# A Strassen-like mixing product: outer sums, weight conversions and loads at planned steps, stores of converted weights on GpSimd's queue, and ScalarE squares in the first block of the last stage

## The chip, the cores and the metric

One core of one Trainium2 chip runs the whole program in one launch. The metric is the device time of an execution in microseconds. Engines are named as the profile does: PE is TensorE (PEld its weight load), DVE is VectorE, ACT is ScalarE, POOL is GpSimd, SP is SyncE, which here only issues DMAs.

## The reference

Three layers follow each other on x of 4 x 3072 x 256.

```python
X = np.fft.rfft(x, axis=1)                      # layer 1: mixing in frequency
Yr = Xr @ w_r - Xi @ w_i + b_r; Yi = Xr @ w_i + Xi @ w_r + b_i
y = irfft(soft_threshold(Yr, Yi, 0.01))
h = np.maximum(x @ w_in, 0.0); u, v = h[..., :512], h[..., 512:]   # layer 2
v_n = (v - mu) / np.sqrt(var + 1e-06)
v_s = np.einsum('ts,bsd->btd', w_spatial, v_n) + b_spatial[None, :, None]
x = (u * v_s) @ w_out
h = x @ w2_in                                    # layer 3
out = (s * np.maximum(h, 0) ** 2 + b) @ w2_out   # w2_in 256 x 2048, w2_out 2048 x 256
```

The einsum with w_spatial (3072 x 3072) against 3072 rows of 4 x 512 columns is the mixing product. The weights of layers 2 and 3 come as 64-bit numbers and have to be converted.

## The kernel before

The program has three stages on TensorE: the frequency layer with the first product of layer 2 (up to some 540 us), the mixing product (to 1811 us), and the last stage, which makes the rest of layer 2 and layer 3 in 24 blocks of 512 columns. All products are done as float32 pairs: ScalarE rounds an operand to its high part, VectorE subtracts to get the low part (called *lows* below), and three passes (high by high, high by low, low by high) go to TensorE.

**The mixing product** (`mixing`, L731) uses Winograd's form of Strassen's scheme twice. The outer scheme has seven products, in the order 1, 5, 2, 6, 3, 7, 4 (`OUTER`, L708); each is again split into quarters a11 to a22 and b11 to b22 of six tiles each, and seven inner products in the order 2, 5, 3, 1, 6, 7, 4 (`INNER`, L717). An inner product runs over NS = 6 contraction tiles. So there are 7 x 7 x 6 = 294 **steps** n, each of 24 matmuls of 128 x 384 columns on four accumulators of two banks (`multiply`, L848). A step is named here by its number; steps 42 to 83 are those of the second outer product, and step 71 is the last of its fifth inner product.

An a tile (128 x 768) and a b tile (128 x 512) of a quarter lie in SBUF and are changed in place by the inner scheme's sums (`sums`, L803, on VectorE, three steps ahead). `high` (L831, ScalarE) and `low` (L836, VectorE) split them two steps ahead. When the last step of an inner product ends, `evacuate` (L866) takes the four accumulators out: VectorE adds an accumulator to a kept tile (called a **fold** below, L874) and POOL's queue stores it to md, or ScalarE copies it to a kept tile (L878). The next step writes the same accumulators, so TensorE waits for it.

A tile that has had its last use is loaded anew for the next outer product. `freed` lists it; `loads` (L782) issues on SyncE's queue the load of the **first term** (L766), and for outer products 5, 6, 3, 7 and 4 of a **second term** (L772) into a staging tile (`st_a`, `st_b`, three buffers each). After three steps `outer_sums(3)` (L796) lets VectorE add or subtract the second term in place, and where OUTER says so (products 5 and 6, the second and fourth in the list) POOL's queue stores the sum for later use (L777).

**Conversions.** 40 halves of the weights of the last stage are converted during the mixing product (`convert_half`, L1254, and `convert`, L133): SyncE loads the 64-bit half into a staging tile, VectorE works nine instructions, ScalarE one, and SyncE's queue stores the result (L162). They take staging buffers of the same `st_a` (raw and result) and `st_b` (three work tiles). In the loop of `run` a conversion is taken up where nothing is to be added or loaded, and worked off in one piece:

```python
            outer_sums(3)
            if conversion and (todo or n % 3 == 2):
                conversion.pop()()
            loads()
            if n >= 6 and not conversion and not added and not todo and n % 3 == 0:
                conversion = [x for x in [convert_half(stage)] if x]
```

Each engine, and each DMA queue, works in the order in which this code issues; nothing is reordered later.

**The last stage** (`output`) goes over blocks n and over k = 0 to 7 in `layer1` (L1080): 12 matmuls to ps_h, ScalarE's relu to r (L1094), VectorE's square (L1095), ScalarE's rounding (L1096) and VectorE's low part (L1097). Two steps later `layer2` uses it. Ahead of it `u_product`, `gate` (L1053 to L1058) and `out_product` of the next block are put in at k = 4 to 6. In block 0 VectorE also adds up the columns of the second weight (`add_columns`, L1132).

Of the kernel before, what the change touches and what calls it, by code (L numbers as in the profile page):

```python
# [27 lines left out]
NS = TQ // 128  # L28
# [7 lines left out]
def f(ap):  # L36
    return ap.bitcast(F32)
# [94 lines left out]

def convert(nc, tile_, raw, dst, n):  # L133

# [26 lines left out]
    def s4():  # L161
        nc.sync.dma_start(out=dst, in_=f(o))  # L162
    return [s0, s1, s2, s3, s4]
# [558 lines left out]


class Stage:

# [5 lines left out]
def mixing(tc, nc, ws, vn, md, sd, convert_half):  # L731
# [7 lines left out]
    q = {}  # L739
# [23 lines left out]
    def load(g, name, i):  # L763
        first, then = OUTER[outer[g]][0 if name[0] == "a" else 2:][:2]
        t = q[name, i]
        nc.sync.dma_start(out=t, in_=source(first, name, i))  # L766
        if then is None:
            return
        op, second, kept = then
        n = t.shape[1]  # L770
        s = banks[2].tile([128, n], F32, tag="st_" + name[0], name="st_" + name[0], bufs=3)
        nc.sync.dma_start(out=s, in_=source(second, name, i))  # L772

        def add():
            nc.vector.tensor_tensor(out=t, in0=t, in1=s, op=getattr(ALU, op))
            if kept:
                nc.gpsimd.dma_start(out=sd[kept][int(name[1]) - 1, int(name[2]) - 1, i], in_=t)  # L777
        added.append((now[0], name[0], add))

    todo = []  # L780

    def loads():  # L782

        n = {"a": 3, "b": 3}
        for _, kind, _ in added:
            n[kind] -= 1
        for x in sorted(todo):
            g, _, i, name = x
            if OUTER[outer[g]][1 if name[0] == "a" else 3] is not None:
                if n[name[0]] <= 0:  # L790
                    continue
                n[name[0]] -= 1
            todo.remove(x)
            load(g, name, i)

    def outer_sums(age):  # L796
        while added and added[0][0] <= now[0] - age:
            added.pop(0)[2]()

# [3 lines left out]
    def sums(n):  # L803

        p, i = INNER[n // NS % 7], n % NS
        a11, a12, a21, a22, b11, b12, b21, b22 = (q.get((x, i)) for x in QUARTERS)
        if p == 2:
# [89 lines left out]
    def run():  # L897
# [12 lines left out]
        for n in range(total):  # L910
# [15 lines left out]
            if ends:  # L926
                evacuate(n, 2)
                evacuate(n, 3)
            outer_sums(3)
            if conversion and (todo or n % 3 == 2):  # L930
                conversion.pop()()
            loads()
            if n >= 6 and not conversion and not added and not todo and n % 3 == 0:
                conversion = [x for x in [convert_half(stage)] if x]
        while True:
            for x in conversion:
                x()
            conversion = [x for x in [convert_half(stage)] if x]
            if not conversion:
                break  # L940
        left.close()
# [10 lines left out]
def output(tc, nc, yd, md, chunks, cd, bs, s_in, b_in, out, finish):  # L952
# [127 lines left out]
    def layer1(n, k):  # L1080
# [13 lines left out]
        nc.scalar.activation(r, ps, AF.Relu)  # L1094
        nc.vector.tensor_mul(r, r, r)  # L1095
        nc.scalar.copy(s[:, 0], r)  # L1096
# [144 lines left out]
def network(ctx, tc, ins, out):  # L1241
# [12 lines left out]
    def convert_half(pool):  # L1254

        if not halves:
            return None
        j, h = halves.pop(0)
        src = chunks[j]
        src = src[:, h, :] if len(src.shape) == 3 else src[:, h * 256:(h + 1) * 256]  # L1260

        def c_tile(tag, shape, dtype):
            tag, bufs = ("st_a", 3) if tag in ("raw", "o") else ("st_b", 3)
            return pool.tile(shape, dtype, tag=tag, name="c_w", bufs=bufs)
        raw = convert_load(nc, c_tile, src, 256)
        return lambda: [step() for step in convert(nc, c_tile, raw, cd[j][:, :, h * 256:(h + 1) * 256], 256)]
    with tc.manual_schedule():
# [29 lines left out]
```

## Time and profile before

| | before |
|---|---|
| median of 3 runs | 3144.45 us (3143.99 to 3144.72) |
| profiled execution, its own time | 3143.22 us |
| span of its profile | 3141.5 us |
| PE busy | 3035.7 us (97%) |
| DVE busy | 2289.4 us (73%) |
| ACT busy | 1395.2 us (44%) |
| POOL busy | 387.9 us (12%) |
| granted clock of TensorE, mean | 0.988 |

The span is the time from the first to the last instruction of the profiled execution. Busy shares are averages over the three stages; TensorE's is near 100% in the settled parts of the last two, so what can be saved there is what a stretch takes beyond its matmuls. The granted clock is a share of 2.4 GHz; where it is 0.5 TensorE ran at 1.2 GHz.

### The profile page before, as it was taken

The page shows a single profiled execution, that of the slowest core. Times are in us where ns is not written, and L with a number is a line of the kernel's source. Part 1 is how long each engine was busy: PE and PEld are TensorE (multiplying, and loading weights), DVE is VectorE, ACT ScalarE, POOL GpSimd, SP SyncE. Part 2 cuts the span into 40 slices and gives each one's busy share as a digit, 9 for nine tenths or more (in the row PEclk, how much of TensorE's full clock was granted, in tenths as well). Part 3 has the DMA queues.
Part 4 walks back from the last instruction along what each step waited for, and adds up shares of the span by engine and source line. Part 5 has one row for each costly group of instructions (what it writes and reads, how often), then busy time and mean ns, then how long its engine had stood idle before and what let it go on. Part 6 is the DMA issues. An engine that isn't in the chain of part 4 may idle for free.

```text
span 3141.5 us, 42065 instructions
## 1 busy us (share of the span) xinstructions
PE 3035.7 (97%) x16026; PEld 2744.0 (87%) x16026; DVE 2289.4 (73%) x3291; ACT 1395.2 (44%) x2069; POOL 387.9 (12%) x488
## 2 busy tenths in 40 slices
PE   6999997999999999999999989999999999999999
PEld 4889885999999999999999978888888888888887
DVE  5888998797878888888878866566565665655664
ACT  5777766433334333434434324344343434334343
POOL 2665544021000210000000000000000000000000
PEclk8999999999999999999999999999999999999999
DMA  8987768586456957467471621202111211102010
GB/s 242 287 288 242 236 215 289 185 330 264 157 194 217 353 214 231 143 209 276 141 256 40 241 101 49 83 31 74 57 61 44 76 42 60 71 31 101 31 37 14
DMA packets 217602, 488.01 MB, mean 155 GB/s; under 512 B 21748, under 2 KB 66616, under 8 KB 217400
## 3 DMA queue, kind: packets, MB, share of 16 engines
q1 hardware_dynamic: 185624, 358.23, 34.1%
q0 software_dynamic: 31776, 127.11, 11.0%
q8 instruction: 125, 2.05, 0.3%
q14 instruction: 77, 0.63, 0.1%
HBM read 322.72 MB, written 162.53 MB: 154 GB/s over the span
## 4 chain that ended last, share of the span: by engine, by line
PE 61%; issue 19%; DVE 11%; DMA 5%; ACT 2%; POOL 1%; SPq 0%; POOLq 0%; ACTq 0%; DVEq 0%
PE oacc L1111 16%; PE ps_h L1090 16%; PE acc L857 13%; PE ps_o L1070 4%; PE ps_u L1045 4%; PE ps_m L414 3%; PE ps_vp L579 2%; PE ps_z L340 1%; POOL md L875 1%; DMA st_b<-vn 1%; PE ps_g L367 1%; DMA c_w<-in_moe_w_in_dram 1%; DMA st_a<-in_moe_w_spatial_dram 1%; DVE a_hl L838 1%; DVE bn L592 1%
## 5 line engine op out<-in xcount | busy, mean ns | idle before, releaser
L857 PE MATMUL acc<-a_hl,b_hl 128*128 128x384 f32 x7056 | 1238.8, 336 | 32.8 <-DVE kept L874 12.0
L857 PEld LDWEIGHTS acc<-a_hl,b_hl 128*128 128x128 f32 x7056 | 1233.0, 189 | 38.6 <-ACT kept L878 12.8
L1090 PE MATMUL ps_h<-x_hl,w 128*128 128x512 f32 x2304 | 555.9, 390 | 6.2 <-ACT r L1094 6.2
L1111 PE MATMUL oacc<-q_hl,w 128*128 128x512 f32 x2304 | 555.1, 390 | 1.6 <-ACT q_hl L1096 0.8
L1090 PEld LDWEIGHTS ps_h<-x_hl,w 128*128 128x128 f32 x2304 | 434.3, 189 | 97.0 <-ACT r L1094 6.6
L1111 PEld LDWEIGHTS oacc<-q_hl,w 128*128 128x128 f32 x2304 | 433.3, 188 | 92.1 <-ACT q_hl L1096 1.2
L834 ACT CAST a_hl<-a 128x768 fp32r<-128x768 f32 x253 | 211.6, 836 | 522.3 <-PE acc L857 443.8
L1095 DVE TENSOR_TENSOR r<-r 128x1024 f32<-128x1024 f32 x192 | 234.9, 1224 | 214.8 <-ACT r L1094 214.1
L1097 DVE TENSOR_TENSOR q_hl<-r,q_hl 128x1024 fp32r<-128x1024 f32 x192 | 235.2, 1225 | 214.3 <-ACT q_hl L1096 214.3
L1094 ACT ACTIVATE r<-ps_h 128x1024 f32<-128x1024 f32 x192 | 197.1, 1027 | 325.9 <-PE ps_h L1090 325.9
L838 DVE TENSOR_TENSOR a_hl<-a,a_hl 128x768 fp32r<-128x768 f32 x253 | 241.3, 954 | 137.4 <-ACT a_hl L834 137.0
L1096 ACT CAST q_hl<-r 128x1024 fp32r<-128x1024 f32 x192 | 201.6, 1050 | 287.5 <-DVE r L1095 287.5
L838 DVE TENSOR_TENSOR b_hl<-b,b_hl 128x512 fp32r<-128x512 f32 x295 | 201.9, 685 | 0.0
L834 ACT CAST b_hl<-b 128x512 fp32r<-128x512 f32 x295 | 181.8, 616 | 0.0
L875 POOL DMA_DIRECT2D md<-kept x112 | 60.5, 540 | 828.9 <-DVE kept L874 824.5
L579 PE MATMUL ps_vp<-win,y_hl 128*128 128x512 f32 x576 | 149.8, 396 | 1.6 <-ACT y_hl L479 1.2
L1045 PE MATMUL ps_u<-y_hl,w 128*128 128x512 f32 x576 | 138.2, 389 | 0.0
L1070 PE MATMUL ps_o<-g,w 128*128 128x512 f32 x576 | 135.2, 390 | 1.7 <-DVE m L1053 0.8
L1070 PEld LDWEIGHTS ps_o<-g,w 128*128 128x128 f32 x576 | 107.9, 188 | 25.5 <-DVE m L1053 1.5
L1045 PEld LDWEIGHTS ps_u<-y_hl,w 128*128 128x128 f32 x576 | 108.2, 188 | 22.4
L579 PEld LDWEIGHTS ps_vp<-win,y_hl 128*128 128x128 f32 x576 | 101.2, 189 | 20.2 <-ACT y_hl L479 1.6
L414 PE MATMUL ps_m<-w_hi,xh 128*128 128x256 f32 x376 | 106.4, 283 | 8.6 <-DVE mt L426 8.6
(142 smaller groups left out, 3657.5 us busy)
## 6 DMA issues: line engine op xcount, KB each, us to landing
a<-in_moe_w_spatial_dram SPq DMA_DIRECT2D x144, 384.0 KB, 5.0
b<-vn SPq DMA_DIRECT2D x168, 256.0 KB, 5.4
md<-kept POOLq DMA_DIRECT2D x112, 384.0 KB, 5.6
m<-md SPq DMA_DIRECT2D x42, 1024.0 KB, 6.5
st_a<-in_moe_w_spatial_dram SPq DMA_DIRECT2D x72, 384.0 KB, 6.7
vn<-vr POOLq DMA_DIRECT2D x96, 256.0 KB, 4.4
s<-a POOLq DMA_DIRECT2D x48, 384.0 KB, 5.8
x_f<-in_x_dram SPq DMA_DIRECT2D x32, 384.0 KB, 6.3
```

What stands on the lines that cost most here:

```text
L414: nc.tensor.matmul(ps[:, n, :], lhs, rhs[:, ri, h, :], start=c == 0, stop=False)
L579: nc.tensor.matmul(ps, y[:, a, k, o:o + 128], win[k][:, w, :], start=c == 0, stop=c == 5)
L834: nc.scalar.copy(s[:, 0, :], t)
L838: sub(s[:, 1, :], term.pop((kind, n)), f(s)[:, 0, :])
L857: nc.tensor.matmul(acc[d][:, h, 0:TH], b[:, m, d * 128:(d + 1) * 128], a[:, w, h * TH:(h + 1) * TH], start=fresh and i == 0 and c == 0, st ...
L1045: nc.tensor.matmul(ps[:, d, 0:TB], win[k][:, a, o:o + 128], y[:, w, k, :], start=c == 0, stop=c == 5)
L1070: nc.tensor.matmul(ps[:, h, 0:TB], wo[k // 2][:, a, o:o + 128], g[:, w, k, :], start=c[h] == 0, stop=c[h] == 11, skip_group_check=n == 0)
L1090: nc.tensor.matmul(ps[:, e, 0:TB], w[:, a, o:o + 128], x[:, i, j, :], start=c == 0, stop=c == 5)
L1095: nc.vector.tensor_mul(r, r, r)
L1096: nc.scalar.copy(s[:, 0], r)
L1097: nc.vector.tensor_sub(s[:, 1], r, f(s)[:, 0])
L1111: nc.tensor.matmul(ps[:, h, 0:TB], w[:, a, o:o + 128], s[:, i, e, :], start=ff == 0 and c == 0, stop=ff == 2 * NP - 1 and c == 2)
```

## The change

In the mixing product the rule of the loop is replaced by tables of steps. `CONVERSIONS` lists the 40 steps after which a half is converted (42 times the outer product's place, 6 times the inner one's, and the tile); its load is issued when one of the next four steps is in the list. `ADD_AT` gives for each quarter the step at which its outer sum is made, counted from the start of the outer product before (so 42 and more lie in the outer product that uses it). First terms are loaded as soon as a tile is free. Second terms are loaded from `LEAD` = 3 steps before their sum, as staging buffers are free, in the order of those steps. The store of a converted half goes to GpSimd's queue. In the last stage ScalarE squares r in block 0, VectorE in the other blocks as before.

```diff
-def convert(nc, tile_, raw, dst, n):
+def convert(nc, tile_, raw, dst, n, queue=None):
...
-        nc.sync.dma_start(out=dst, in_=f(o))
+        (queue or nc.sync).dma_start(out=dst, in_=f(o))
...
+CONVERSIONS = {42 * g + 6 * p + i for g, p, i in (
+    (0, 1, 1), (0, 1, 3), (0, 1, 4), (0, 2, 1), (1, 2, 1), (1, 2, 4), (1, 3, 0), (1, 3, 1),
...
+ADD_AT = {"a12": 18, "b21": 30, "a21": 36, "b12": 36, "a22": 42, "b11": 42, "b22": 45, "a11": 48}
+LEAD = 3
...
         if then is None:
-            return
+            state[name, i] = g
+        else:
+            second_terms.append((g, name, i, then))
+
+    def load_second(g, name, i, then):
...
-        added.append((now[0], name[0], add))
+        added.append((g, name, i, add))
...
+    def due(g, name, i):
+        return 42 * (g - 1) + ADD_AT[name] + i
...
+        for x in sorted(second_terms, key=lambda x: due(*x[:3])):
+            g, name, i, _ = x
+            if n[name[0]] > 0 and now[0] >= due(g, name, i) - LEAD:
                 n[name[0]] -= 1
-            todo.remove(x)
+                second_terms.remove(x)
+                load_second(*x)
+        for g, _, i, name in sorted(todo):
             load(g, name, i)
...
-    def outer_sums(age):
-        while added and added[0][0] <= now[0] - age:
-            added.pop(0)[2]()
+        todo.clear()
+
+    def outer_sums(everything=False):
+        for x in list(added):
+            g, name, i, add = x
+            if everything or due(g, name, i) <= now[0]:
+                added.remove(x)
+                add()
+                state[name, i] = g
...
-            outer_sums(3)
-            if conversion and (todo or n % 3 == 2):
+            outer_sums()
+            if n in CONVERSIONS:
+                outer_sums(True)
                 conversion.pop()()
-            loads()
-            if n >= 6 and not conversion and not added and not todo and n % 3 == 0:
-                conversion = [x for x in [convert_half(stage)] if x]
...
+            loads(len(conversion))
+            if not conversion and any(m in CONVERSIONS for m in range(n + 1, n + 5)):
+                conversion.append(convert_half(stage))
...
-        nc.vector.tensor_mul(r, r, r)
+        if n == 0:
+            nc.scalar.square(r, r)
+        else:
+            nc.vector.tensor_mul(r, r, r)
...
-        return lambda: [step() for step in convert(nc, c_tile, raw, cd[j][:, :, h * 256:(h + 1) * 256], 256)]
+        return lambda: [step() for step in convert(nc, c_tile, raw, cd[j][:, :, h * 256:(h + 1) * 256], 256, nc.gpsimd)]
```

How the instructions stand. First SyncE's queue at the end of the first outer product, where the quarters of product 5 come in (b22 are first terms, L766 before and L779 now; st_a and st_b second terms, L772 before and L790 now). Before:

```order
L766 DMA b22_6341<-vn3_72 128x512
L772 DMA st_b_9163<-vn1_70 128x512
L766 DMA b22_6342<-vn3_72 128x512
L772 DMA st_b_9166<-vn1_70 128x512
L766 DMA b22_6343<-vn3_72 128x512
L772 DMA st_b_9211<-vn1_70 128x512
```

and now, from the last first terms on:

```order
L779 DMA a22_6340<-in_moe_w_spatial_dram 128x768
L779 DMA b22_6346<-vn3_72 128x512
L790 DMA st_b_9136<-vn0_69 128x512
L790 DMA st_a_9138<-in_moe_w_spatial_dram 128x768
L790 DMA st_b_9182<-vn0_69 128x512
L790 DMA st_a_9184<-in_moe_w_spatial_dram 128x768
L790 DMA st_b_9224<-vn0_69 128x512
L790 DMA st_a_9226<-in_moe_w_spatial_dram 128x768
```

Before, a first term and its second term alternate, so that the next first term stands behind a load that needs a staging buffer; now the first terms come early and the second terms of a22, b11, b22 and a11 follow by themselves.

Next VectorE ahead of the fold that ends step 71 (L838 and L869 are lows, L825 and L856 sums of the inner scheme, L874 and L905 folds). Before:

```order
L838 TENSOR_TENSOR a_hl<-a_6359,a_hl 128x768
L838 TENSOR_TENSOR b_hl<-b_6371,b_hl 128x512
L144 TENSOR_SCALAR c_w<-c_w 128x256
L145 TENSOR_SCALAR c_w<-c_w 128x256
L146 TENSOR_SCALAR c_w<-c_w 128x256
L149 TENSOR_SCALAR c_w<-c_w 128x256
L150 TENSOR_TENSOR c_w<-c_w 128x256
L151 TENSOR_SCALAR c_w<-c_w 128x256
L154 TENSOR_SCALAR c_w<-c_w 128x256
L155 SCALAR_TENSOR_TENSOR c_w<-c_w 128x256
L159 SCALAR_TENSOR_TENSOR c_w<-c_w 128x256
L825 TENSOR_TENSOR a_6361<-a_6337,a_6361 128x768
```

and now:

```order
L869 TENSOR_TENSOR a_hl<-a_6359,a_hl 128x768
L869 TENSOR_TENSOR b_hl<-b_6371,b_hl 128x512
L856 TENSOR_TENSOR a_6361<-a_6337,a_6361 128x768
L905 TENSOR_TENSOR kept<-acc,kept 128x768 x2
L869 TENSOR_TENSOR a_hl<-a_6360,a_hl 128x768
```

The conversion of nine instructions has left this place; before, the fold came right after the a-sum that closes the first list.

Last ScalarE at the start of block 0 of the last stage. Before:

```order
L1094 ACTIVATE r<-ps_h 128x1024
L1096 CAST q_hl<-r 128x1024
L1094 ACTIVATE r<-ps_h 128x1024
L1096 CAST q_hl<-r 128x1024
L1094 ACTIVATE r<-ps_h 128x1024
```

and now:

```order
L1120 ACTIVATE r<-ps_h 128x1024
L1122 ACTIVATE r<-r 128x1024
L1125 CAST q_hl<-r 128x1024
L1120 ACTIVATE r<-ps_h 128x1024
L1122 ACTIVATE r<-r 128x1024
```

The square stands on ScalarE's own list between relu and rounding, eight times; before, rounding waited there for VectorE.

## Rows read from the trace of the kernel before

**Rows 1.** Busy time in stretches; columns named in the first line.
```profile
core 0: us, PE busy (x) PEld busy (x) DVE busy (x) ACT busy (x) POOL busy (x), PEclk, DMA share, GB/s
1640.00:1743.00 103.00, 103.00 (x597) 103.00 (x596) 85.11 (x148) 44.58 (x68) 2.17 (x4) 1.00 0.21 69
...
693.35:737.42 44.07, 36.05 (x193) 35.12 (x193) 30.87 (x40) 13.95 (x20) 13.24 (x25) 0.92 1.03 415
1064.54:1109.21 44.67, 36.27 (x194) 35.34 (x193) 31.07 (x40) 13.95 (x20) 12.95 (x24) 0.92 1.03 414
833.11:898.10 64.99, 57.86 (x313) 56.93 (x313) 50.75 (x90) 21.86 (x34) 6.47 (x12) 0.95 0.65 213
1225.69:1238.77 13.08, 10.15 (x50) 9.69 (x49) 10.98 (x21) 3.01 (x5) 2.16 (x4) 0.87 0.60 199
...
1825.91:1886.69 60.78, 51.75 (x206) 40.75 (x204) 41.51 (x41) 18.19 (x19) 0.00 (x0) 0.89 0.12 43
1943.82:1998.22 54.40, 54.40 (x241) 45.06 (x240) 31.14 (x27) 22.03 (x22) 0.00 (x0) 1.00 0.18 63
```

**Rows 2.** Waits of PE, 693.35 to 737.42 us: total, times, longest.
```profile
PE acc L857 <- DVE kept L874: 5.3, 1, 5.3
```

**Rows 3.** Timeline of DVE: start, length, what; in brackets idle time and releaser.
```profile
729.52 0.69 DVE L775 TENSOR_TENSOR b<-b,st_b 128x512 f32<-128x512 f32 x1 [1.62 <-DMA st_b<-vn]
730.13 1.81 DVE L874 TENSOR_TENSOR kept<-acc,kept 128x768 f32<-128x768 f32 x2
731.87 0.95 DVE L838 TENSOR_TENSOR a_hl<-a,a_hl 128x768 fp32r<-128x768 f32 x1
732.73 0.69 DVE L838 TENSOR_TENSOR b_hl<-b,b_hl 128x512 fp32r<-128x512 f32 x1
733.33 0.95 DVE L874 TENSOR_TENSOR kept<-acc,kept 128x768 f32<-128x768 f32 x1
```

**Rows 4.** Timeline of all engines around the end of step 71.
```profile
853.50 0.42 SPq L129 DMA_DIRECT2D c_w<-in_moe_w_in_dram  x1
...
857.57 0.29 DVE L144 TENSOR_SCALAR c_w<-c_w 128x256 uint32<-128x256 uint32 x1 [2.12 <-DMA c_w<-in_moe_w_in_dram]
...
860.17 0.95 DVE L825 TENSOR_TENSOR a<-a,a 128x768 f32<-128x768 f32 x1
...
861.03 1.81 DVE L874 TENSOR_TENSOR kept<-acc,kept 128x768 f32<-128x768 f32 x2
...
862.13 6.16 PE L857 MATMUL acc<-a_hl,b_hl 128*128 128x384 f32 x26 [2.85 <-ACT a_hl L834]
```

**Rows 5.** Waits of SP's queue and of DVE, 540 to 1812 us.
```profile
SPq L162 <- DVE c_w L159: 443.7, 40, 26.2
...
DVE c_w L144 <- DMA c_w<-in_moe_w_in_dram: 16.7, 6, 4.9
```

**Rows 6.** DMA issues, 540 to 1812 us: count, KB each, median us to landing.
```profile
st_a<-in_moe_w_spatial_dram SPq DMA_DIRECT2D x72, 384.0 KB, 6.7
...
st_b<-vn SPq DMA_DIRECT2D x48, 256.0 KB, 6.1
```

**Rows 7.** Costliest groups of the page: count, busy us, mean ns, idle before.
```profile
L1095 DVE TENSOR_TENSOR r<-r 128x1024 f32<-128x1024 f32 x192 | 234.9, 1224 | 214.8 <-ACT r L1094 214.1
...
L1094 ACT ACTIVATE r<-ps_h 128x1024 f32<-128x1024 f32 x192 | 197.1, 1027 | 325.9 <-PE ps_h L1090 325.9
...
L875 POOL DMA_DIRECT2D md<-kept x112 | 60.5, 540 | 828.9 <-DVE kept L874 824.5
```

**Rows 8.** Timeline of all engines in block 0 of the last stage.
```profile
1856.71 1.22 DVE L1095 TENSOR_TENSOR r<-r 128x1024 f32<-128x1024 f32 x1
...
1861.53 1.22 DVE L1008 TENSOR_TENSOR m<-m,bias 128x1024 f32<-128x1024 f32 x1
1862.66 1.22 DVE L1053 SCALAR_TENSOR_TENSOR m<-ps_u,m 128x1024 f32<-128x1024 f32 x1
1863.91 1.04 ACT L1057 CAST g<-m 128x1024 fp32r<-128x1024 f32 x1 [4.89 <-DVE m L1053]
1864.86 1.02 ACT L1094 ACTIVATE r<-ps_h 128x1024 f32<-128x1024 f32 x1
...
1865.93 5.49 PE L1090 MATMUL ps_h<-x_hl,w 128*128 128x512 f32 x12 [6.18 <-ACT r L1094]
```

More of the change, by code (lines that the diff above doesn't have):

```diff
@@ L767, in load @@
         if then is None:
-            return
+            state[name, i] = g
+        else:
+            second_terms.append((g, name, i, then))
+    def load_second(g, name, i, then):
+        t = q[name, i]
         op, second, kept = then
@@ L777, in add, with loads @@
                 nc.gpsimd.dma_start(out=sd[kept][int(name[1]) - 1, int(name[2]) - 1, i], in_=t)
-        added.append((now[0], name[0], add))
+        added.append((g, name, i, add))
     todo = []
[L782 to L791, printed above, removed]
+    def due(g, name, i):
+        return 42 * (g - 1) + ADD_AT[name] + i
+    second_terms = []
+    def loads(taken):
+        n = {"a": 3 - taken, "b": 3}
+        for _, name, _, _ in added:
+            n[name[0]] -= 1
+        for x in sorted(second_terms, key=lambda x: due(*x[:3])):
+            g, name, i, _ = x
+            if n[name[0]] > 0 and now[0] >= due(g, name, i) - LEAD:
                 n[name[0]] -= 1
-            todo.remove(x)
+                second_terms.remove(x)
+                load_second(*x)
+        for g, _, i, name in sorted(todo):
             load(g, name, i)
-    def outer_sums(age):
-        while added and added[0][0] <= now[0] - age:
-            added.pop(0)[2]()
+        todo.clear()
[6 more added lines that the diff above has]
+                state[name, i] = g
+    state = {}
     sub, add = nc.vector.tensor_sub, nc.vector.tensor_add
@@ L805, in sums @@
         p, i = INNER[n // NS % 7], n % NS
+        assert all(state[x, i] == n // (7 * NS) for x, use in FIRST_USE.items() if use == n // NS % 7)
         a11, a12, a21, a22, b11, b12, b21, b22 = (q.get((x, i)) for x in QUARTERS)
@@ L928, in run @@
                 evacuate(n, 3)
-            outer_sums(3)
-            if conversion and (todo or n % 3 == 2):
+            outer_sums()
+            if n in CONVERSIONS:
+                outer_sums(True)
                 conversion.pop()()
-            loads()
-            if n >= 6 and not conversion and not added and not todo and n % 3 == 0:
-                conversion = [x for x in [convert_half(stage)] if x]
[L935 to L940, printed above, removed]
+            loads(len(conversion))
+            if not conversion and any(m in CONVERSIONS for m in range(n + 1, n + 5)):
+                conversion.append(convert_half(stage))
         left.close()
```

4 rows, old and new, of the table CONVERSIONS are left out of this document.

## The prediction

> **What bounds the kernel now.** I read the table of stretches first, since TensorE is the engine that the rest serves. In an undisturbed stretch of the mixing product (the first line of [rows 1]), 103.00 us show 597 matmuls; less the three that only reach in over the edges, that is 173 ns each, so a step of 24 matmuls takes 4.16 us. The next four lines are cut at the starts of steps. They hold 8, 8, 13 and 2 steps (each count is one more than 24 times that, for the same reason), which undisturbed would be 33.28, 33.28, 54.08 and 8.32 us. They took 44.07, 44.67, 64.99 and 13.08: **10.8, 11.4, 10.9 and 4.8 us too long**, 37.9 us in all. The first two stretches lie where the quarters of outer products 2 and 4 in the list (numbers 5 and 6) are put in; their DMA share is 1.03 at 415 GB/s, so the DMA engines are full there and elsewhere not (0.65, 0.60). Two lines belong to the last stage. A settled block took 54.40 us for 240 matmuls, 0.2267 us each; block 0, up to block 1's first matmul of that layer, took 60.78 us for 204, which at the same pace are 46.2 us: **14.5 us too long**.
>
> What ends the waits? In the first stretch TensorE waits 5.3 us at once for VectorE's fold of an accumulator [rows 2]. VectorE's timeline there [rows 3] shows why: the outer sum that stands ahead of the fold waits 1.62 us for its second term from DMA, as do those before it. VectorE takes its work in order, so a late load of an operand needed much later stops the fold needed now. In the third stretch [rows 4] it is a converted weight: SyncE issues the raw half's load at 853.50, VectorE idles 2.12 us for it, converts until 860.17, and only then come the a-sum and the fold; TensorE stands 2.85 us until 862.13 (the row names ScalarE's rounding, which waits for that a-sum and ends with the first fold). The load was that late because SyncE's queue had waited for the conversion before: its store waits for VectorE, 443.7 us over 40 stores, up to 26.2 [rows 5], and every load stands behind it.
>
> **The change part by part.** *Part A, outer sums and their loads.* One a tile is 384 KB, one b tile 256 [rows 6]. At both transitions 48 tiles are read, their second terms read, and the sums written, so a pair of tiles moves 3 x 640 = 1920 KB. In the old order the pairs of steps 28 to 39 also share their time with four md stores of 384 KB per six steps: 2176 KB a step against 4.16 us x 415 GB/s = 1686 KB. Twelve such steps owe 5880 KB, 14.5 us of DMA; TensorE lost 10.8 and 11.4. The new table takes the second term and the sum of a22, b11, b22 and a11 past step 41. Counted by issue: steps 33 to 38 ask for 11,904 KB (12 second terms, 12 first, 9 sums, md) against 10,116, 4.4 us too much; steps 39 to 44 for 10,624, the debt is 5.7 us; steps 45 to 50 for 7,680, which clears it. So the debt falls from 14.5 to 5.7 us. The lead of three steps, 12.5 us, about covers a second term that lands in 6.7 us [rows 6] plus this debt. Two things remain. In steps 45 to 47 there are two b sums a step on three buffers, so a buffer must come round in 6.2 us, and its load alone takes 6.1 [rows 6]. And VectorE itself is full: by the spacing of starts (0.86 us an a tile, 0.60 a b tile [rows 3]) a step there has the lows 1.46, the sums of the next phase 1.46, an a sum 0.86 and two b sums 1.20, so 4.98 us against 4.16; steps 48 to 50 have 4.38. That is 3.1 us. I leave **6 us at each transition**: these 3.1 and half of the debt. Gain 22.2 - 12 = **10.2 us**. Ends: 2 us left each (VectorE's overhang partly absorbed by the two steps that the split runs ahead), gain 18; or 11 left, gain 0.
>
> *Part B, conversions and their stores.* Same 40 conversions, 2.60 us of VectorE each from start to next start [rows 4]; 20 stand now in steps without sums, where 1.46 + 2.60 = 4.06 fits into 4.16, the others in steps that overrun by 0.8 to 1.7 us but mostly stand apart from each other. None stands any longer just ahead of a fold, and SyncE no longer waits for VectorE there. What is queued behind the moved store is POOL's: stores of md and of sums, which nobody needs within 10 us. POOL's issue takes 540 ns [rows 7]; 40 more, at up to twice that for a store in twice as many pieces, are 43 us of an engine idle most of the stage. Of 10.9 + 4.8 = 15.7 us I leave 1.7, for runs of three and four conversions in which one buffer must be stored and reloaded between: gain **14.0 us**, ends 9 and 15.7.
>
> The Trainium skill, "SBUF — State Buffer", section "Who interferes with whom", speaks against this part: a DMA issued by GpSimd can stand still while VectorE holds the port pair that the two share, and tensor_scalar, of which a conversion has six, is among the operations that may hold it. By it the store, and so the next raw load, would come later; this is a rival below.
>
> *Part C, squares of block 0.* Eight multiplications of 1224 ns leave VectorE and come to ScalarE. Its price there is not in the trace; the nearest row is ScalarE's relu on the same tile, 1027 ns, against 1224 on VectorE [rows 7], and I take 1.03. ScalarE was busy 18.2 of 60.8 us [rows 1], so 8.2 more fit. VectorE was busy 41.5, and worse at the end: the gate of block 1 starts at 1862.66, behind four squares that stood between it and the last idle time; only then can ScalarE round g and read ps_h, and TensorE has stood 6.18 us at 1865.93 [rows 8]. Without them the gate comes 4 x 1.13 = 4.5 us earlier. The granted clock of block 0 is 0.89 [rows 1]: after these waits TensorE ran at 1.2 GHz instead of 2.4 for a while (12 matmuls from 1865.93 took 5.49 us [rows 8], 2.8 more than at full pace), and with the waits that goes too. 4.5 + 2.8, and 1.7 for a square that no longer queues behind column sums: **9.0 us**, which leaves 5.5 us, the serial gate, rounding and out product. Ends 4 and 12. The skill's "ScalarE: Activation LUTs", section "Rules for kernel authors", would keep a multiplication on VectorE; the relu row above is the shorter one here, so by the trace the rule does not hold for this tile.
>
> **Sum:** 10.2 + 14.0 + 9.0 = 33.2 us. The profiled execution took 3143.22 us, so 3110.0; the median of the three runs is 1.2 above it, so **3111 us**. With the good ends 18 + 15.7 + 12 = 45.7: 3099. With the bad ends 0 + 9 + 4 = 13: 3131.
>
> **The rivals.**
> R1, *the stall only moves*: the transitions' waits reappear at steps 44 to 53, as the same bytes must pass. For it: DMA share 1.03 now; against it: the debt worked out above is 0.4 of the old one. A gains 0: 3121 us.
> R2, *GpSimd's queue is late*: each store waits until VectorE's burst is over, up to 3 us, and the third and later conversions of a run (seven of them) wait about 2 us each. For it: no row shows a POOL issue amid conversions, since SyncE stored their results. Against it: the md stores issue in 540 ns [rows 7] with VectorE busy beside them. B gains 0: 3125 us. The rule of the skill quoted above would work in this way.
> R3, *ScalarE becomes the queue of block 0*: relu, square and rounding in one order delay the next relu, C gains 0: 3120 us. Against it: 3.1 us of ScalarE a step of 5.4.
> R4, *slower*: sums at fixed steps stop VectorE for each late load. A second term that lands in L lets three buffers serve one step every (L + 0.7) / 3 us, and over 24 steps of a transition the excess is 24 x ((L + 0.7) / 3 - 4.16). From L = 15 us on this costs more than all gains. At 16, 33.8 us a transition against 11 now, so 45 lost and 23 gained: 3166 us. Against it: 6.7 us measured with the DMA engines full.
> That the planned steps don't take effect is excluded by the order shown above.
>
> **How the numbers follow.** All three gain: 0.60. R1 0.20, R3 0.08, R2 0.07; two or three of these at once, which comes near no change, 0.02; R4 0.03. A measurement of this kernel tells about 0.2% (6.3 us) from no change. So faster 0.95, same 0.02, slower 0.03. The range from 3099 to 3131 holds the forecast with its bounds and R1 to R3 alone, and leaves out R4 and the combinations.
>
> **What would show it.** Right: stretches of steps 35 to 42 and 119 to 126 at 4.2 us a step with 2 to 8 us of wait some ten steps later; no wait of SyncE for VectorE at the weight store; VectorE's waits for c_w loads from 16.7 to under 5 us; block 0 near 52 us and its clock near 1.0. Wrong: over 8 us lost at a transition (A), POOL issues of the weight store over 1.5 us or VectorE idle ahead of conversions in runs (B), ScalarE's square over 1.3 us (C).

## The result, and the profile after

The changed kernel took **3114.58 us** (median of four runs, 3111.30 to 3117.46) against 3144.59 us (3143.99 to 3145.51) for the kernel before, run beside it: ratio 0.9904, 95% interval 0.9887 to 0.9921. The profiled execution took 3111.30 us with a span of 3109.3. The kernel before had 3143.22 and 3141.5, so the two traces differ by 32.2 us.

The stretches of [rows 1] in the changed kernel, cut at the same places of the program: steps 35 to 42, 47 to 54, 119 to 126, 131 to 138, 66 to 78, 83 to 90, 155 and 156, and block 0. Columns are named in the first line.

```profile
core 0: us, PE busy (x) PEld busy (x) DVE busy (x) ACT busy (x) POOL busy (x), PEclk, DMA share, GB/s
691.70:726.45 34.75, 33.92 (x193) 33.16 (x193) 27.20 (x35) 13.96 (x20) 10.79 (x20) 1.00 1.01 384
743.13:781.78 38.65, 35.73 (x193) 32.82 (x193) 38.55 (x53) 16.60 (x25) 9.21 (x17) 1.00 0.89 306
1052.09:1086.13 34.04, 33.86 (x193) 33.22 (x193) 27.26 (x36) 13.95 (x20) 10.79 (x20) 1.00 1.01 382
1102.79:1141.45 38.66, 35.77 (x193) 32.81 (x193) 38.56 (x53) 16.62 (x25) 9.21 (x17) 1.00 0.88 311
827.55:883.05 55.50, 54.66 (x313) 54.03 (x313) 45.55 (x71) 21.37 (x32) 7.90 (x14) 1.00 0.70 238
899.70:935.60 35.90, 34.06 (x193) 33.13 (x193) 34.33 (x72) 16.40 (x27) 5.57 (x9) 1.00 0.41 144
1208.00:1216.33 8.33, 8.33 (x49) 8.33 (x49) 7.00 (x9) 2.71 (x4) 2.17 (x4) 1.00 0.69 242
1803.11:1854.69 51.58, 48.32 (x206) 39.21 (x205) 31.88 (x33) 27.14 (x27) 0.00 (x0) 0.97 0.15 52
```

Steps 35 to 42 fell from 44.07 to 34.75 us and 119 to 126 from 44.67 to 34.04 (undisturbed: 33.28), with the DMA engines nearly as full as before (share 1.01 against 1.03, 384 and 382 GB/s against 415 and 414). The granted clock is 1.00 in all stretches but block 0. What is left at a transition lies later, in steps 47 to 54 and 131 to 138: 38.65 and 38.66 us. There VectorE is busy 38.55 us, all the time. Steps 66 to 78 take 55.50 us instead of 64.99 (the wait of [rows 4] is gone), 155 and 156 8.33 instead of 13.08, and block 0 takes 51.58 instead of 60.78.

The waits of TensorE over the mixing product in the changed kernel (total, times, longest):

```profile
PE acc L888 <- ACT kept L909: 6.1, 6, 1.4
PE acc L888 <- ACT vr L617: 5.2, 1, 5.2
PE acc L888 <- DVE kept L905: 3.1, 5, 0.8
```

The single wait of 5.3 us for a fold [rows 2] is gone; no fold is now late by more than 0.8 us. The middle row is the start of the stage.

VectorE in the changed kernel, the timeline that answers to [rows 3] (in brackets the idle time and its releaser):

```profile
727.92 0.68 DVE L793 TENSOR_TENSOR b<-b,st_b 128x512 f32<-128x512 f32 x1
728.88 0.96 DVE L793 TENSOR_TENSOR a<-a,st_a 128x768 f32<-128x768 f32 x1 [0.28 <-DMA st_a<-in_moe_w_spatial_dram]
729.76 0.95 DVE L869 TENSOR_TENSOR a_hl<-a,a_hl 128x768 fp32r<-128x768 f32 x1
730.63 0.68 DVE L869 TENSOR_TENSOR b_hl<-b,b_hl 128x512 fp32r<-128x512 f32 x1
735.30 0.69 DVE L793 TENSOR_TENSOR b<-b,st_b 128x512 f32<-128x512 f32 x1 [3.99 <-DMA st_b<-vn]
737.04 0.96 DVE L793 TENSOR_TENSOR a<-a,st_a 128x768 f32<-128x768 f32 x1 [1.04 <-DMA st_a<-in_moe_w_spatial_dram]
737.92 0.95 DVE L869 TENSOR_TENSOR a_hl<-a,a_hl 128x768 fp32r<-128x768 f32 x1
```

Second terms are still late: VectorE idles 0.28 + 3.99 + 1.04 = **5.31 us** here. No fold stands right behind these sums, so TensorE feels nothing yet. It feels it at steps 47 to 54, which took 38.65 us instead of 33.28: **5.3 us** lost, the undisturbed steps among them left out. Experiments below show that these two numbers belong together. Two sums a little earlier, at 716.80 and 719.17 us, wait as well, 1.34 and 1.69 us, and a fold does stand right behind them: step 42 loses 1.1 us. That is the old stall in small.

How the longest of these waits comes about can be read from the issue of its load on SyncE's queue:

```profile
721.37 0.33 SPq L790 DMA_DIRECT2D st_b<-vn  x1
```

The load left the queue at the start of step 42 and landed 13.9 us later, at 735.28. VectorE stood at the sum from 731.31 on, early in step 44: of the lead of three steps, 12.5 us, only 9.9 were there.

Landing times from 703 to 740 us, where before and after have the DMA engines full (count, KB each, median us):

```profile
st_a<-in_moe_w_spatial_dram SPq DMA_DIRECT2D x8, 384.0 KB, 11.5
...
st_b<-vn SPq DMA_DIRECT2D x7, 256.0 KB, 12.3
```

Over the whole stage the median for st_a is 4.8 us, against 6.7 in [rows 6].

The queues, [rows 5] in the changed kernel:

```profile
SPq L129 <- DMA cd<-c_w: 157.8, 19, 25.7
POOL cd L162 <- ACT b_hl L865: 426.5, 37, 60.1
DVE c_w L144 <- DMA c_w<-in_moe_w_in_dram: 3.2, 3, 2.1
```

SyncE's 443.7 us of waiting at the weight store have become 426.5 us on GpSimd's list, where nobody is in a hurry behind it. SyncE still waits 157.8 us in all, in the first line, before it loads a raw half: for the landing of a store, whose buffer the load takes. VectorE waits 3.2 us for this weight's raw halves instead of 16.7.

Where the 32.2 us come from, in us beyond 4.16 a step (start of a step's first matmul to the next one's, steps over by 0.1 or more) and, for block 0, in whole time:

| | before | after | gain |
|---|---|---|---|
| steps 28 to 54 and 113 to 138 (part A) | 22.2 | 12.9 | 9.3 |
| other steps from 1 to 156 (part B) | 15.7 | 4.7 | 11.0 |
| block 0 (part C) | 60.8 | 51.6 | 9.2 |
| start of the mixing product | 540.1 | 537.7 | 2.3 |
| the rest | | | 0.4 |

### The profile page after: what moved, and what is told of

Read it like the earlier page. It is cut to its first block, busy times and chain, and to the rows that moved or that the text cites. A ratio compares the mean times of both kernels' runs of the same rounds, so it can differ in the third digit from the quotient of the medians.

```text
span 3109.3 us, 42026 instructions
## 1 busy us (share of the span) xinstructions
PE 3029.3 (97%) x16026; PEld 2732.7 (88%) x16026; DVE 2279.6 (73%) x3283; ACT 1405.4 (45%) x2077; POOL 415.8 (13%) x528
## 4 chain that ended last, share of the span: by engine, by line
PE 75%; DVE 13%; issue 7%; ACT 3%; DMA 2%; POOL 1%; ACTq 0%; POOLq 0%; SPq 0%; DVEq 0%
PE acc L888 26%; PE oacc L1140 16%; PE ps_h L1116 16%; PE ps_o L1096 4%; PE ps_u L1071 4%; PE ps_m L414 3%; PE ps_vp L579 2%; DVE a_hl L869 1%; PE ps_z L340 1%; PE ps_g L367 1%; DVE b_hl L869 1%; DVE bn L592 1%; PE ps_y L462 1%; DVE kept L905 1%; DVE y_sb L470 1%
## 5 line engine op out<-in xcount | busy, mean ns | idle before, releaser
L888 PEld LDWEIGHTS acc<-a_hl,b_hl 128*128 128x128 f32 x7056 | 1223.6, 188 | 27.5 <-ACT kept L909 10.7
L1124 DVE TENSOR_TENSOR r<-r 128x1024 f32<-128x1024 f32 x184 | 224.9, 1222 | 206.9 <-ACT r L1120 206.8
L869 DVE TENSOR_TENSOR a_hl<-a,a_hl 128x768 fp32r<-128x768 f32 x253 | 241.1, 953 | 131.7 <-ACT a_hl L865 131.3
L869 DVE TENSOR_TENSOR b_hl<-b,b_hl 128x512 fp32r<-128x512 f32 x295 | 201.6, 683 | 0.0
L905 DVE TENSOR_TENSOR kept<-acc,kept 128x768 f32<-128x768 f32 x112 | 103.6, 951 | 36.7 <-PE acc L888 35.1
L906 POOL DMA_DIRECT2D md<-kept x112 | 60.8, 543 | 442.9 <-DVE kept L905 442.4
```

The lines of the kernel that those rows point to most:

```text
L869: sub(s[:, 1, :], term.pop((kind, n)), f(s)[:, 0, :])
L888: nc.tensor.matmul(acc[d][:, h, 0:TH], b[:, m, d * 128:(d + 1) * 128], a[:, w, h * TH:(h + 1) * TH], start=fresh and i == 0 and c == 0, st ...
```

## The experiments

The kernel before, run beside them, had 3142.80 us for the first four experiments told here, 3143.31 for the next three and the one on b22 alone, and 3143.34 for the others. "Lost" means beyond 4.16 us a step.

**Part C alone** (kernel before, and this):

```diff
-        nc.vector.tensor_mul(r, r, r)
+        if n == 0:
+            nc.scalar.square(r, r)
+        else:
+            nc.vector.tensor_mul(r, r, r)
```

> The kernel before with the squares of block 0 on ScalarE and nothing else. If the three parts of the change are independent, as the prediction has it, this gains part C alone: block 0 falls from 60.8 us to 51 to 53 us, the mixing product is as before, and the median is 9 us below the kernel before, 3135 to 3137 us. The rival is that block 0's late VectorE work comes from the stage ahead (late weights or folds) and that the square only helps together with the rest: then less than 4 us.

3133.64 us, ratio 0.9973 (0.9963 to 0.9982), 9.2 below (3135 to 3137 was counted from 3144.5, not from the 3142.80 beside it). Block 0 took 52.0 us and the mixing product lost 49.4 against 48.3. So part C stands by itself and is worth what it was taken for. ScalarE's square, by line, min/median/max in ns:

```profile
L1096 ACT ACTIVATE r<-r x8: 1056/1062/1067, 1829.6 to 1876.2; 128x1024 f32<-128x1024 f32 x8
```

**The store on GpSimd's queue alone** (kernel before, and this):

```diff
...
-        nc.sync.dma_start(out=dst, in_=f(o))
+        (queue or nc.sync).dma_start(out=dst, in_=f(o))
...
```

> The kernel before with the stores of converted weights on GpSimd's queue; conversions and sums keep the old rule. Theory 'order': TensorE loses time because a conversion stands on VectorE just ahead of a fold; that order is unchanged here, so the stretches of steps 66 to 78 and 155 to 156 lose at most 4 us less than their 10.9 and 4.8 us, and the median is 3140 to 3144 us. Rival 'queue': SyncE's queue, held by the store, makes the raw halves late; without the store both stretches are clean and the median is 3128 to 3132 us.

3139.99 us, ratio 0.9991 (0.9981 to 1.0): at most a few us, and far from the rival's 3128 to 3132. Steps 55 to 112 lost 8.1 instead of 10.9, steps 139 to 156 3.2 instead of 4.8, and VectorE's wait for raw halves fell only to 12.6 us: the conversion still stands just ahead of the fold.

**The planned steps with the store on SyncE's queue** (changed kernel, and this):

```diff
-        return lambda: [step() for step in convert(nc, c_tile, raw, cd[j][:, :, h * 256:(h + 1) * 256], 256, nc.gpsimd)]
+        return lambda: [step() for step in convert(nc, c_tile, raw, cd[j][:, :, h * 256:(h + 1) * 256], 256)]
```

> The changed kernel with the stores of converted weights back on SyncE's queue; the planned steps stay. Theory 'order' alone would have the same time as the changed kernel, 3113 to 3117 us. Theory 'order and queue': in runs of three and four conversions each load of a raw half stands behind the store of the one before, which waits for VectorE, so the load comes 3 to 5 us late at some seven places, VectorE stands still for it, and folds and the next product wait: 3135 to 3155 us, with waits of VectorE for c_w loads of 20 us and more in all (3.9 us in the changed kernel).

3153.01 us, ratio 1.0038 (1.0023 to 1.0053): **slower than the kernel before**, and some 40 us from the changed kernel (10.2 above the kernel before, and 30.0 below it). Steps 55 to 112 lost 28.4 us, against 4.1 in the changed kernel, and VectorE waited 40.1 us for raw halves (22.6 and 17.5 us for the two weights) against 3.9. Its timeline of SyncE's queue and VectorE:

```profile
934.96 0.52 SPq L162 DMA_DIRECT2D cd<-c_w  x1
935.57 1.43 SPq L129 DMA_DIRECT2D c_w<-in_moe_w_in_dram  x1
939.43 0.29 DVE L144 TENSOR_SCALAR c_w<-c_w 128x256 uint32<-128x256 uint32 x1 [2.92 <-DMA c_w<-in_moe_w_in_dram]
...
942.18 0.52 SPq L162 DMA_DIRECT2D cd<-c_w  x1
942.79 0.56 SPq L129 DMA_DIRECT2D c_w<-in_moe_w_in_dram  x1
```

Each raw half is loaded only when the store of the half before has been issued, so a run of conversions goes store, load, landing, conversion, in one chain. The new order has such runs, and it works only with the store on the second queue: the two edits of part B belong together.

**The old kind of rule for the conversions** (changed kernel, but a conversion is taken up at every third step where nothing is to be added, and worked off when a load comes up):

```diff
-            if n in CONVERSIONS:
-                outer_sums(True)
+            if conversion and (todo or n % 3 == 2 or any(n >= due(*y[:3]) - LEAD for y in second_terms)):
...
-            if not conversion and any(m in CONVERSIONS for m in range(n + 1, n + 5)):
-                conversion.append(convert_half(stage))
+            if n >= 6 and not conversion and not added and n % 3 == 0 and all(n + 2 < due(*y[:3]) - LEAD for y in second_terms):
+                conversion = [x for x in [convert_half(stage)] if x]
...
```

> The changed kernel with conversions taken up by the old kind of rule (every third step, where nothing is added and no second term is near) instead of the planned steps; planned sums, GpSimd stores and the ScalarE squares stay. If the plan of the conversions has a worth of its own, waits come back at the folds after a conversion (steps 71, 72, 77, 78, 155, 156), 5 to 11 us in all, and the median is 3119 to 3126 us. The rival is that the sums' plan and the queue do everything: 3113 to 3117 us.

3122.00 us, ratio 0.9936 (0.9921 to 0.9951). The waits of steps 71, 72, 77, 78, 155 and 156 came back (steps 55 to 112 lost 10.1 us and 139 to 156 lost 2.5, against 4.1 and 0 in the changed kernel), and VectorE waited 16.7 us for raw halves, as in [rows 5]. The transitions lost 7.0 and 7.3 us, against 6.8 and 6.1. Its median lies 20.8 us below the kernel before, the changed kernel's 30.0; in the traces its mixing product lost 7.5 us more (35.2 against 27.8). So the list of steps is worth 7 to 9 us, and the gain at the transitions hardly depends on it.

**The outer sums as early as in the old order** (changed kernel, other table):

```diff
-ADD_AT = {"a12": 18, "b21": 30, "a21": 36, "b12": 36, "a22": 42, "b11": 42, "b22": 45, "a11": 48}
+ADD_AT = {'a12': 18, 'b21': 27, 'a21': 33, 'b12': 27, 'a22': 39, 'b11': 33, 'b22': 39, 'a11': 24}
```

> The changed kernel with the sums at about the steps of the old order: a11 24, b21 27, b12 27, a21 33, b11 33, a22 39, b22 39; first terms still apart from second ones. Theory 'debt': twelve steps ask again for 2176 KB where 1686 KB pass, second terms come late, VectorE stands at them ahead of the folds, and steps 29 to 42 and 113 to 126 lose 9 us or more each: 3122 to 3140 us. Rival 'interleaving': the old loss came from first terms that stood in the queue behind loads without a free buffer; then each transition stays below 7 us, and the time within 4 us of the changed kernel.

3138.53 us, ratio 0.9985 (0.9976 to 0.9995). The transitions lost 16.3 and 16.5 us, more than before the change. VectorE's waits for second terms of a, over the stage:

```profile
DVE a L793 <- DMA st_a<-in_moe_w_spatial_dram: 25.6, 11, 4.9
```

The changed kernel has 6.8 us there. The DMA engines were full for 104 us around the first transition (share 1.02 from 652.36 to 756.00 us). So the rival is out: first terms apart from second ones do not help by themselves, and putting sums past step 41 is what part A gains by. That it is the bytes asked for in the same steps which make the loads late is worked out from the counts; no run changed the bytes and left the steps of the sums alone.

**The last sums later still** (changed kernel):

```diff
-ADD_AT = {"a12": 18, "b21": 30, "a21": 36, "b12": 36, "a22": 42, "b11": 42, "b22": 45, "a11": 48}
+ADD_AT = {"a12": 18, "b21": 30, "a21": 36, "b12": 36, "a22": 42, "b11": 42, "b22": 48, "a11": 50}
```

> The changed kernel with the sums of b22 due at 48 instead of 45 and those of a11 at 50 instead of 48. In the changed kernel steps 47 to 54 and 131 to 138 lose 5.3 us each. Theory 'VectorE': steps 45 to 50 hold more VectorE work (4.98 and 4.38 us) than a step lasts (4.16); moved, steps 45 to 47 hold 4.38, 48 to 50 about 4.0 and 51 to 53 4.7 us, so the overhang falls from 3.1 to about 2.2 us and comes where no fold by VectorE follows: each transition loses 1 to 3 us instead of 5.3, and the median is 3 to 8 us below the changed kernel's 3114.6. Rival 'buffers': late loads of second terms are the cause; they come as late as before, and the loss stays above 4 us at each transition.

3115.62 us, ratio 0.9909 (0.9894 to 0.9924), no gain: a miss. Steps 46 to 54 lost 2.8 instead of 5.3, as expected, but steps 57 and 58 lost 4.1 and steps 141 and 142 lost 4.3, where the moved sums of a11 now meet conversions. VectorE's waits for second terms had not become shorter (5.7 and 5.9 us); the smaller loss comes from the work that was put off.

**The same, with six conversions moved** out of their way, to steps 59, 143, 160, 163, 183 and 185 (changed kernel):

```diff
...
+CONVERSIONS = {262, 7, 9, 10, 265, 268, 13, 270, 271, 272, 143, 278, 283, 157, 158, 285, 160, 163, 183, 185, 59, 60, 61, 62, 73, 75, 78, 79, 80, 85, 86, 87, 91, 94, 223, 97, 226, 228, 229, 230}
+ADD_AT = {'a12': 18, 'b21': 30, 'a21': 36, 'b12': 36, 'a22': 42, 'b11': 42, 'b22': 48, 'a11': 50}
```

> As the run with later sums, and six conversions moved: those after steps 55, 58, 81, 88, 139 and 181 to 183, 59, 160, 163, 143 and 185, so that the runs of four become runs of three and no conversion follows the crowded steps 51 to 54 at once. If the remaining losses at steps 83, 84, 89 and 90 (2.6 us) and at 57 and 58 come from VectorE's crowding and from the reloaded buffer in runs of four, they go: 3 to 6 us below the run with later sums, 3101 to 3108 us. The rival is that the moved conversions press on other places (steps 141 to 144, 160 to 167, 183 to 186), with no gain over the run with later sums.

**3108.39 us** (3107.68 to 3109.80), ratio 0.9887 (0.9871 to 0.9904): the fastest kernel here that computes the whole result, 7.2 us below the run with later sums and just above the 3108 expected at most. The mixing product lost 23.2 us against 27.8: steps 83, 84, 89 and 90 lose nothing any more and 57 and 58 0.2 us, but steps 65 and 66 lose 2.9 instead of 1.1.

**One step further** (that kernel, the conversion after step 59 moved to 99, and the column sums of block 0 spread otherwise):

```diff
-                add_columns(2 * (NP - 1 - k))
+                add_columns((16, 12, 9, 6, 4, 4, 2, 0)[k])
...
```

> The run with six moved conversions, with the conversion after step 59 moved to 99 as well, so that a run of three stays there, and the column sums of block 0 taken one or two earlier so that the gate of block 1 finds VectorE free. If runs of four and the sums ahead of the gate cost what the profiles say (steps 65 and 66: 2.9 us, of which 1 to 1.5 stay; k = 6 in block 0: 4.8 us too long), 2 to 3.5 us below that run's 3108.4: 3105 to 3107 us. If the waits only move, 3108 us.

3109.77 us, ratio 0.9892 (0.9878 to 0.9907): a miss. Block 0 took 51.0 instead of 51.6 us, and the mixing product lost 24.8; steps 65 and 66 still lost 2.8. Between these two kernels the runs decide nothing.

**The changed kernel once more.**

> The changed kernel unaltered, beside the next run on the same chip. If its scatter (3111.3 to 3117.5 us) comes from the first stage, where both kernels have the same program, the mixing product's excess in the profile is 27.9 us within 2 us, and the median 3112 to 3117 us.

3113.92 us (3112.86 to 3115.28), ratio 0.9904 (0.9888 to 0.9921). The mixing product lost 27.5 us (27.8 before) and block 0 took 51.7; its start was at 541.0 us instead of 537.7. The stage ahead of it, the same program in all these kernels, is where the two executions differ; over the traces of this document it ends between 537.7 and 541.9 us.

**What the 5.3 us after a transition are.** Three kernels ask. First, b22 in products 5 and 6 takes its second operand from a resident tile (changed kernel):

```diff
+        if name == "b22" and op == "subtract" and kept:
+            s = q["b12", i]
+        else:
```

> The changed kernel, but in outer products 5 and 6 the sum of b22 takes the resident tile b12 as its second operand, so that 12 loads of 256 KB and their use of three buffers fall away while VectorE does the same work; the second term of b22 is left out of the result. Theory 'VectorE': steps 47 to 54 lose 4.5 to 5.5 us as in the changed kernel (5.3). Theory 'buffers' (half of the debt, as the prediction charged): the loss falls to 3 us or less.

3115.50 us (one run), steps 47 to 54 lost 5.3 us as before. I first read this as VectorE's work alone. That was wrong: the trace shows VectorE's waits for the late loads of b11 and a22 untouched (4.0 us at 737 us, as in the changed kernel), since the loads that were taken away come after them. So two more kernels ask, first without all late loads:

```diff
+        if kept and name in ("a22", "b11", "b22", "a11"):
+            s = t
+        else:
```

> The changed kernel, but in products 5 and 6 the outer sums of a22, b11, b22 and a11 add the tile to itself instead of a second term: 24 loads of second terms at each of the two transitions are left out (those values are therefore other ones), VectorE's instructions stay. Theory 'overhang alone' (VectorE has more work than 4.16 us a step in steps 45 to 53): VectorE's 3.99 us of idle time at 735 us goes, and steps 47 to 54 still lose 4.5 to 5.5 us at each transition. Theory 'half of it is the DMA debt, which makes VectorE enter these steps late' (as the prediction had it): 2 to 3.5 us are left at each.

and, changed kernel again,

```diff
-            nc.vector.tensor_tensor(out=t, in0=t, in1=s, op=getattr(ALU, op))
+            if not (kept and name == "b22"):
+                nc.vector.tensor_tensor(out=t, in0=t, in1=s, op=getattr(ALU, op))
```

> The changed kernel, but the six sums of b22 in products 5 and 6 are left out on VectorE, while their second terms are loaded and their stores made as before (b22 then holds its first term alone). DMA is as full as in the changed kernel, VectorE has 0.60 us a step less in steps 45 to 50. 'Overhang alone': 47 to 54 lose 1.5 to 2.5 us instead of 5.3, since 6 x 0.60 = 3.6 us of work are gone. 'Debt': 3.5 us or more are left, as the late loads still hold VectorE.

3103.95 and 3105.86 us (one run each). Without the loads, VectorE's timeline and the stretch of steps 47 to 54 (columns as above) are

```profile
733.50 0.68 DVE L796 TENSOR_TENSOR b<-b 128x512 f32<-128x512 f32 x1
734.10 0.95 DVE L796 TENSOR_TENSOR a<-a 128x768 f32<-128x768 f32 x1
734.97 0.95 DVE L872 TENSOR_TENSOR a_hl<-a,a_hl 128x768 fp32r<-128x768 f32 x1
735.84 0.68 DVE L872 TENSOR_TENSOR b_hl<-b,b_hl 128x512 fp32r<-128x512 f32 x1
```

```profile
745.74:779.01 33.27, 33.27 (x193) 33.27 (x193) 33.17 (x45) 16.66 (x24) 7.56 (x14) 1.00 0.47 173
```

VectorE never idles and is busy for the whole stretch (33.17 of 33.27 us), with the same sums as in the changed kernel, and so is TensorE. **Nothing is lost** in steps 43 to 54, nor in 127 to 138. Both theories had something left: both missed. With the loads but without six sums, VectorE's waits at the end of the first transition (726 to 742 us) are

```profile
DVE b L794 <- DMA st_b<-vn: 4.0, 1, 4.0
DVE a L794 <- DMA st_a<-in_moe_w_spatial_dram: 2.1, 2, 1.6
```

6.1 us, and steps 47 to 54 lost 1.8; with step 46, where some of it already shows, 2.6. At the second transition it was 5.8 us, and 1.8 or 2.0. By its number that is what 'overhang alone' expected, but the kernel without the loads has ruled that theory out: its hit is luck. One reading fits all of them: VectorE's work up to step 53 just fits into TensorE's time, so each us that it idles for a late load is lost, and each us of work taken away is given back.

| | VectorE idle, us | work less, us | idle less work | lost in steps 46 to 54 or 129 to 138 |
|---|---|---|---|---|
| changed kernel, first transition | 5.3 | 0 | 5.3 | 5.3 |
| second transition | 5.2 | 0 | 5.2 | 5.3 |
| changed kernel again, first | 5.7 | 0 | 5.7 | 5.7 |
| no b22 sums, first | 6.1 | 6 x 0.60 | 2.5 | 2.6 |
| no b22 sums, second | 5.8 | 6 x 0.60 | 2.2 | 2.0 |
| no second loads, both | 0 | 0 | 0 | 0 |

The idle column is VectorE's waits for st_a and st_b in the 16 to 18 us that begin at the end of step 42 (126 the second time). This reading was formed after the runs, from these rows, and no kernel was built to test it. Traces that were not used for it bear it out, as these kernels leave the sums where the changed kernel has them:

| | VectorE idle, us | lost in the same steps |
|---|---|---|
| changed kernel again, second | 5.0 | 5.3 |
| b22 from a resident tile, first and second | 5.3, 5.1 | 5.3, 5.2 |
| old kind of rule, first and second | 5.7, 6.0 | 5.7, 6.2 |
| store on SyncE's queue, first and second | 7.6, 6.1 | 7.7, 6.2 |

In the three kernels with later sums, 2.6 to 3.1 us less is lost than VectorE idles. That is near the price of the two a and two b sums (2.9 us) that they put off past step 51, but which sums count was not worked out ahead. Not tested is what would make the loads come in time, as a longer lead or a fourth staging buffer.

## Why the prediction was right, and where it was not

**The time**: 3111 us forecast, 3114.58 and 3113.92 measured, 3111.30 in the profiled execution; the forecast that all three parts gain came true. The three terms gave 33.2 us and measured 29.5 (9.3 + 11.0 + 9.2), as the medians do (30.0 below the kernel before). The profiled execution came closer to the forecast than that because its mixing product began 2.3 us earlier, which is scatter that the prediction did not count: that part is luck.

**Part A**, 10.2 forecast, 9.3 measured. The order was right: steps 35 to 42 nearly undisturbed, a loss some ten steps later. The early-sums kernel shows that the place of the sums is what gains. But the step "these 3.1 and half of the debt", 6 us a transition, was put together wrongly. After step 42 VectorE idled about as long as the *whole* debt (5.7 forecast, 5.3 and 5.2 us), and TensorE lost all of it; VectorE's overhang of 3.1 us cost nothing by itself: with no loads to wait for, the same work made TensorE lose nothing. The prediction had this at its good end, where the steps that the split runs ahead absorb a part; they absorbed all. The two errors cancel but for 0.8 and 0.1 us at 6.8 and 6.1 left, which is luck. That the idle time comes near 5.7 is weak evidence for the debt itself: with steps 40 and 41 it is 8.3 and 8.6 us. The lead was misjudged too: "about covers" set 12.5 us against 6.7 + 5.7, and the load shown above took 13.9 us, and VectorE was there after 9.9. The way of the loss was also another: the longest of TensorE's waits in steps 47 to 54 is not for a fold but for ScalarE's copy L909, as ScalarE's rounding waits for VectorE's inner sums (14.3 us in five waits for L841) and the copy stands behind the rounding.

**Part B**, 14.0 forecast, 11.0 measured: the mechanism right, the term mis-sized. "I leave 1.7" was 4.7. One place is a run of four conversions, where a single raw half is late in the changed kernel:

```profile
894.38 0.29 DVE L144 TENSOR_SCALAR c_w<-c_w 128x256 uint32<-128x256 uint32 x1 [2.06 <-DMA c_w<-in_moe_w_in_dram]
...
897.58 0.67 POOL L162 DMA_DIRECT2D cd<-c_w  x1 [5.62 <-ACT b_hl L865]
```

Steps 83 and 84 lose 1.5 us behind it. In the others VectorE works without a gap: steps 89 and 90 (1.1 us, behind the last of four conversions in a row among inner sums and lows), 66 and 78 (1.4 us; step 66 lost its 1.1 before as well) and 11 and 12 (0.6 us, undisturbed before). So the 1.7 that the prediction left for reloaded buffers in runs came nearly true (1.5), and the other 3.2 us, where conversions in a row delay the end of an inner product, it put at nothing. One of its signs of being wrong, VectorE idle ahead of conversions in runs, did show, but small: 3.9 us in all (3.2 of them for this weight). That conversions must not stand ahead of a fold is shown by the kernel with the old rule, and that the queue matters by the store on SyncE's queue; the prediction priced the two edits together, and rightly, since either without the other gains little (2.8 us) or loses.

**Part C**, 9.0 forecast, 9.2 measured, alone and in the whole. Against [rows 8], in the changed kernel:

```profile
1836.88 1.41 DVE L1161 TENSOR_TENSOR w_acc<-w_acc,w 128x512 f32<-128x512 f32 x2
1838.21 1.22 DVE L1079 SCALAR_TENSOR_TENSOR m<-ps_u,m 128x1024 f32<-128x1024 f32 x1
1839.46 1.04 ACT L1083 CAST g<-m 128x1024 fp32r<-128x1024 f32 x1 [3.75 <-DVE m L1079]
1839.48 6.76 PE L1096 MATMUL ps_o<-g,w 128*128 128x512 f32 x22 [2.86 <-DVE m L1079]
```

TensorE waits 2.86 us instead of 6.18, still for the gate, with column sums ahead of it. Spreading those otherwise gave 0.6 us. Term by term the sum fits less well: the gate came 1.65 us sooner after the start of the block (35.10 us against 36.75) and not 4.5, and TensorE's wait there shrank by 3.3; its other waits shrank by 2.4 us (1.7 forecast) and its busy time, at a granted clock of 0.97 instead of 0.89, by 3.4 (2.8 forecast). The errors cancel, which is luck. ScalarE's square took 1060 ns (1057 to 1063), 1.03 forecast, against VectorE's 1224 [rows 7]: the rule of the Trainium skill, "ScalarE: Activation LUTs", section "Rules for kernel authors", that keeps a multiplication on VectorE (it gives its reason for bf16), does not hold for this float32 tile.

**The rivals.** R1 (the stall moves, A gains nothing): it moved, at some 60% of its size (6.8 and 6.1 of 10.8 and 11.4 us). R2 (GpSimd's queue late): in the changed kernel, min/median/max of the weight store's issue in ns,

```profile
L162 POOL DMA_DIRECT2D cd<-c_w x40: 672/677/688, 580.4 to 1756.7; - x40
```

and 2.5 us to landing in the median (4.9 at most), against 2.6 us from SyncE's queue. The weight store comes when its own conversion is over, so it does not test the case that the Trainium skill describes in "SBUF — State Buffer", section "Who interferes with whom", where VectorE's tensor_scalar can hold up GpSimd. But the prediction was wrong that no row shows GpSimd issuing amid conversions. The timeline of the kernel before has one near its end:

```profile
1738.29 0.29 DVE L145 TENSOR_SCALAR c_w<-c_w 128x256 uint32<-128x256 uint32 x1
1738.47 0.54 POOL L875 DMA_DIRECT2D md<-kept  x1 [0.33 <-DVE c_w L144]
1738.49 0.29 DVE L146 TENSOR_SCALAR c_w<-c_w 128x256 f32<-128x256 f32 x1
1738.82 0.29 DVE L149 TENSOR_SCALAR c_w<-c_w 128x256 uint32<-128x256 uint32 x1
```

Beside three tensor_scalar instructions the issue took the usual 0.54 us [rows 7], and these took their usual 0.29; two more such stores, at 921.47 and 1764.35 us, are alike. So the rule does not show in these three places, and with this row R2 would have had a smaller chance. R3 (ScalarE the queue of block 0): ScalarE was busy 27.1 of 51.6 us and TensorE waited 0.4 us for it in block 0; so not by itself, though VectorE waited 1.87 us for ScalarE's rounding just ahead of the column sums and the gate shown above. R4 (slower): nearer than the prediction held. Against its 15 us it put 6.7 us "measured with the DMA engines full", which was the median of the whole stage. In the full stretch a second term of b landed in 12.3 us (median), still below 15. The table with sums some steps earlier lost 16 us a transition, all that part A had gained and more.

## What to carry to other kernels

Price a late operand where it is felt: on VectorE here, which works in order, 5.0 to 7.7 us of idle time passed through one to one (5.2 to 7.7 us lost) as its work filled TensorE's time, and work taken away was given back. So add up idle time and work over the whole stretch rather than look at the wait's neighbour. Take a landing time for a congested stretch from that stretch, not from the median of the stage. A queue that both waits for compute and carries loads turns a dense plan into a chain; move the waiting store off it before planning denser work.

## What was not expected

Full DMA engines cost TensorE little by themselves here: in steps 35 to 42 they ran at share 1.01 and 384 GB/s, and the eight steps took 34.75 us, 1.5 more than undisturbed; before, at 1.03 and 415 GB/s, they took 44.07. The difference is whether a sum with a late operand stands ahead of a fold that is due. And moving only the weight store back to SyncE's queue turned a kernel 30 us faster into one 10 us slower than before.
